# Cosine attention and a low-rank mixer: batch 1 in key tiles of 128, batch 2's quarter slots together, other planned distances, a narrower last piece

## The chip, the cores and the metric

The kernel runs on one core of a Trainium2 chip. The metric is the device time of one execution in microseconds. Before the change it is 580.38 us, the median of six runs that lie between 580.11 and 580.61. The engines are named as in the profile: PE is the tensor engine, PEld its weight loads, DVE the vector engine, ACT the scalar engine, POOL and SP the engines that here mostly issue DMAs.

## What is computed

```python
# q, k, v: (8 batches, 12 heads, 448 rows, 64), float32; tau = 0.1
q_n = q / (norm(q) + 1e-6);  k_n = k / (norm(k) + 1e-6)
attn = softmax(q_n @ k_n.T / tau)
x = attn @ v                       # heads side by side: (8, 448, 768)
# U: (448, 32), V: (32, 448), w_ch1: (768, 3072), w_ch2: (3072, 768)
h = x.T @ U @ V                    # mixes the 448 rows through rank 32
u = x + h.T
out = u + relu(u @ w_ch1) @ w_ch2
```

The kernel works in bfloat16 with float32 sums. Since the rows of q and k have length one, the kernel takes exp of the scores without their maximum.

## The kernel before

**A planner writes the order.** The program first collects operations (`Op`), each with an engine, an assumed duration, the operations that it depends on, and the buffers (`Slot` of a `Ring`) that it takes and gives back. `Plan.run` then runs a list scheduling over the five engines and emits the instructions in the order of planned starts. On the chip each engine keeps that order; if an operand comes later than planned, the engine stands still and all that is behind it waits. PE has several streams in a fixed priority: transposes, score bursts, value products, low-rank sums, and last the MLP (`pe_mlp`), which fills what the others leave. DVE, ACT and SP take the ready operation of lowest `prio`. POOL has one stream, `pool_q`, in the order of the program text.

**Planned distances.** `ready_at` lets a PE operation start no earlier than the end of an operand from another engine plus 0.1 plus `op.safe`, and the same for a buffer that comes free. `plan.safe` is set before operations are added: 0.1 for the start, 0.8 while batch 1's loads and norms are added, then (lines 1140 to 1147) 0.6 for batch 1's attention, 0.8 for that of later batches and 0.25 for all MLPs. `LATE`, 8.0, is the planned time from the end of a load's transfer to its landing for q and k of batches from 1 on and for their v (batch 0 has 2.5 and `VLATE`). The transfers themselves are planned in one queue, 1.24 us for a load of q or k.

**Attention.** Heads go in six pairs. Three loads of q and three of k bring four heads each per batch (`load_qk`). `stats` squares, sums and scales them (ACT or DVE; DVE alone for batch 1), with priority 4 from batch 1 on, and batch 1's squares come after the last product of batch 0. `norm` writes normalized q and k; they are transposed on PE for batches 0 and 1 (L477) and by DMA for the rest (L636). A **slot** is one tile of keys of one head pair: two matmuls of 64 rows by 448 columns (L682), one for each head, and one exp over both (L700). Keys are cut in one of two ways:

- For batches below `WIDE` (2) in four tiles of 112 keys: 24 slots a batch.
- From `WIDE` on in three tiles of 128, and a last one of 64 keys, which two pairs share. This **quarter slot** has four matmuls of 64 by 64 tiles (`parts`), and its other half of v is set to zero. That makes 18 full and 3 quarter slots. v then comes in ten loads instead of four (`load_v`), and its tile gets ones and zeros once by `set_v_tiles` (five memsets) instead of `set_v` (one).

Slots are issued in **bursts** (`BURST`: 1, 2, then 3 for each batch), and `groups_of` puts them in order. For batches from `TB` (3) on the three quarter slots come first, as a burst of their own, and their exps go into a ring of their own (`r_tail`); below `TB` the quarter slot stands behind the full ones of its two pairs. From batch 2 on, a burst waits in the plan for a certain MLP product of the batch before. Scores take double PSUM banks from `r_sc`: (0, 1), (2, 3), (4, 5). `values` multiplies exps by v (L727, 16 matmuls of 65 columns for each head, the last column being the sum), taking a bank from `r_av`, `r_av2` or `r_av3`, and DVE divides (L756, L758).

**Low-rank sums and MLP.** `stage0` computes A = x.T U (L811) and adds A V to x: for batch 1 in three column parts with one matmul (L861) and one DVE addition (L875, L870) per tile, each a PE operation waiting for DVE, and then transposes u on PE. Batches 0 and 1, 2 and 3 and so on share 7 row tiles of 128: the even one has three, the odd one four. `mlp` runs 24 x 6 products with the first weight (L938, 384 or 512 columns), relu (L961 on ACT, L963 on DVE), then for each row tile and each half of the 768 columns 24 products with the second weight (L974), a DVE addition (L985) and stores (L999). The last of the 14 x 4 half tiles is cut in two pieces of 192 columns; stores of pieces narrower than 384 columns and of fewer than 112 rows go to ACT's queue, all others to SP's.

**Order around the start.** POOL's stream is: q and k of batch 0, v of batch 0, half of the first weight, q and k of batch 1 with the rest of the first weight between, v of batch 1, the last q and k of batch 1, eight slices of the second weight, then q, k and v of batch 2.

Of the kernel before, what the change touches and what calls it, by code (L numbers as in the profile page):

```python
# [269 lines left out]
def kernel(  # L270
# [18 lines left out]
    NPAIR = H // 2  # L289
    CC = C // 128  # L290
    NC = F // 128
    CH = C // 2
    SC = 4
    SCH = S // SC
# [1 line left out]
    root_tau = float(tau) ** 0.5  # L296
    EPS = 1e-6
    PE_BATCHES = 2
    LATE, VLATE = 8.0, 2.8
    BURST = [1] + [2] + [3] * 6  # L300
    SPOTS = {8: [(6,)] * 7 + [()], 6: [(5, 17), (10,), (6,), (6,), (6,), (6,)]}
    WIDE = 2
    TB = 3
    RAW_KEYS = {(0, 0), (0, 1)}
    FILL = 0.7

# [78 lines left out]
    r_av3 = bank_ring([(5,), (4,), (3,), (2,), (1,), (0,)], 2, (4, D + 8))  # L385
    r_av2 = bank_ring([(5,), (4,), (3,), (2,), (1,), (0,), (6,)], 2, (4, D + 8))
    r_up = bank_ring([(7,), (6,), (5,), (4,), (3,), (2,), (1,), (0,)], 4)
    r_out = bank_ring([(7,), (6,), (5,), (4,)], 4)
    r_warm = bank_ring([(4,)], 1)
    r_sc1 = bank_ring([(0,), (2,), (1,), (3,)], 4)  # L390
# [21 lines left out]
    plan = Plan()  # L412
# [166 lines left out]

    def stats(b, h0, h1, ld, ops, lo, hold=(), then=()):  # L580

        pr = 0.3 + 0.03 * h0 if b == 0 else 4
        inv = Slot(r_inv, sum(1 + 2 * SC if (b, p) in RAW_KEYS else 2 for p in range(h0 // 2, h1 // 2)))
        o, _, _ = scales(b, h0, h1, ld, ops, lo, (0, 1), inv, pr, "ACT/DVE" if b != 1 else "DVE", hold, then)
        for p in range(h0 // 2, h1 // 2):
            o_ = norm(b, p, ld, lo + 2 * p - h0, inv, 2 * p - h0, {0: o, 1: o}, pr, {1: [ops[1]]})
        return o_
# [76 lines left out]
    def scores(b, slots, then=()):  # L664

        off = PAD * (b % 2)
        scs = [Slot(r_sc, 2 if (b, p) in RAW_KEYS else 1) for p, _ in slots]
        sets = {p: got[b, p, "qkT"] for p in members(b, slots)}
        ready = []
        for x in sets.values():  # L670
            ready += x[1]
        ready += then
        into = []
        for p, c in slots:
            of, r, n = (tails, r_tail, 4) if b >= TB and c == SC - 1 else (attns, r_attn, 2 if b < WIDE or p % 2 or b >= TB else 4)
            into.append(of.setdefault((b, p), (Slot(r, n), [])))

        def score():
            for (p, c), sc in zip(slots, scs):
                for hh, q_, n0, w, out in parts(b, p, c, sc):  # L680
                    qkT, r = sets[q_][0], slice(D * hh, D * hh + D)
                    nc.tensor.matmul(out=out, lhsT=qkT.tile.rearrange("p b s -> p (b s)")[r, n0:n0 + w],  # L682
                                     rhs=qkT.tile[r, SC:2 * SC, :].rearrange("p c s -> p (c s)"),
                                     start=True, stop=True)
        kinds = [b >= WIDE and c == SC - 1 for _, c in slots]
        o = plan.add(Op("PE", 0.2 + pe_t(S) * len(slots) + 0.12 * sum(x != y for x, y in zip(kinds, kinds[1:])), score, deps=ready, acq=scs + [x[0] for n, x in enumerate(into) if x not in into[:n]],
                        rel=[x[0] for x in sets.values()]), pe_first if b == 0 else pe_sc)
        o.big = len(slots) > 2
        if o.big:
            bursts.setdefault(b, []).append(o)  # L690
        for (p, c), sc, (attn, exps) in zip(slots, scs, into):
            _, _, (inv, a, scaled) = sets[p]
            if (b, p) in RAW_KEYS:
                for hh in range(2):
                    exps.append(plan.add(Op("ACT", act_t(S, 0.143), lambda sc=sc, c=c, hh=hh, attn=attn, inv=inv, a=a: nc.scalar.activation(  # L695
                        out=attn.tile[0:SCH, c, hh, off:off + S], in_=sc.tile[0:SCH, hh, 0:S], func=AF.Exp,
                        scale=inv.tile[:, 1, a + hh, c:c + 1]), deps=[o, scaled], acq=[attn],
                        rel=[sc, inv], prio=0.1)))
                continue
            exps.append(plan.add(Op("ACT", act_t(2 * S, 0.08), lambda sc=sc, c=c, attn=attn: nc.scalar.activation(  # L700
                out=attn.tile[:, :, off:off + S] if b >= TB and c == SC - 1 else
                attn.tile[0:SCH if b < WIDE else 128, c, :, off:off + S],
                in_=sc.tile[0:SCH if b < WIDE else 128, :, 0:S], func=AF.Exp),
                deps=[o], acq=[attn], rel=[sc], prio=0.1 if b == 0 else 1)))

    def values(b, p, X):
        off = PAD * (b % 2)
        attn, exps = attns[b, p]
        even, kp, tail = attn, SCH, None
        if b >= WIDE:  # L710
            kp = 128
            if b >= TB:
                tail, more = tails[b, p - p % 2]
                exps = exps + more
            elif p % 2:
                even = attns[b, p - 1][0]
                exps = exps + attns[b, p - 1][1]
        last_exp[b] = exps[-1]
        if b == 0 and p == 0:
            last_exp["first"] = [exps[0]]  # L720
        muls = []
        heads = []
        for hh in range(2):
            heads.append((Slot(r_av3 if b >= 3 else r_av2 if BURST[b] > 2 else r_av if b else r_av5 if p == NPAIR - 1 else r_av0, 1), Slot(r_rd, 1)))

        def product(h, hh, t, j, av, start):
            nc.tensor.matmul(out=av.tile[:, t, 0:D + 1],  # L727
                             lhsT=tail.tile[:, hh, 128 * t:128 * (t + 1)] if tail and j == SC - 1 else
                             (attn if j < SC - 1 else even).tile[0:kp, j, hh, 128 * t:128 * (t + 1)],
                             rhs=v_t[b % 2][0:kp, h, j, 0:D + 1], start=start, stop=(j == SC - 1),  # L730
                             skip_group_check=ends)
        ends = b == 0 and p == NPAIR - 1
        ready = attn_set + v_set[b]
        if ends:
            for j in range(SC):
                for hh, (av, rd) in enumerate(list(heads)):
                    h = 2 * p + hh

                    def fn(h=h, hh=hh, j=j, av=av):
                        for t in range(4):  # L740
                            product(h, hh, t, j, av, j == 0 and t == 0)
                    o = plan.add(Op("PE", 4 * 0.033, fn, deps=[exps[j]] + got[b, h, "v"] + ready,
                                    acq=[av] if j == 0 else [], rel=[attn] if j == SC - 1 else []), pe_av)
                    if j == SC - 1:
                        heads[hh] += (o,)
        for hh in range(2):
            h = 2 * p + hh
            av, rd = heads[hh][:2]
            o = heads[hh][-1]
            for t in () if ends else range(4):  # L750
                for j in range(SC):
                    first, last = t == 0 and j == 0, t == 3 and j == SC - 1
                    o = plan.add(Op("PE", 0.033 if b < 2 else 0.0305, lambda t=t, j=j, h=h, hh=hh, av=av: product(h, hh, t, j, av, j == 0),
                        deps=exps + got[b, h, "v"] + ready if first else (), acq=[av] if first else [],
                        rel=([attn, tail] if tail else [attn] if even is attn else [attn, even]) if last else []), pe_av)
            r = plan.add(Op("DVE", 0.20, lambda av=av, rd=rd: nc.vector.reciprocal(  # L756
                out=rd.tile, in_=av.tile[:, :, D:D + 1]), deps=[o], acq=[rd], prio=1))
            muls.append(plan.add(Op("DVE", dve_t(256), lambda av=av, rd=rd, h=h: nc.vector.tensor_mul(  # L758
                X.tile[:, :, h * D:(h + 1) * D], av.tile[:, :, 0:D],
                rd.tile.to_broadcast([128, 4, D])), deps=[r],  # L760
                acq=[X], rel=[av, rd], prio=1)))
        last_av[b, p] = o
        return muls
# [153 lines left out]
    def mlp(b, us, uT, ut):  # L917
# [4 lines left out]
        work = [(i, t, c0, c0 + CH) for i, t in enumerate(tiles) for c0 in (0, CH)]  # L922
        if b == B - 1:
            i, t, c0, c1 = work.pop()
            mid = (c0 + c1) // 2
            work += [(i, t, c0, mid), (i, t, mid, c1)]
            us[i].uses += 1
            us[i].left += 1
# [39 lines left out]
        for group in groups:  # L968
# [12 lines left out]
            for (i, t, c0, c1), mm in zip(group, mms):  # L981
# [6 lines left out]
                for bb in (b - par, b - par + 1):  # L988
# [3 lines left out]
                        continue  # L992
                    for nn, j, p0, p1 in segments(lo - o0, hi - o0):
                        r0 = nn + o0 - 128 * t
                        by = "ACT" if w < CH and p1 - p0 < SCH else "SP"
                        O.uses += 1
                        O.left += 1
                        plan.add(Op(by, 0.1, lambda bb=bb, j=j, p0=p0, p1=p1, r0=r0, O=O, c0=c0, c1=c1, by=by:
# [139 lines left out]
    w2_ops.append(load_w2(len(w2_ops), 2 * NW))  # L1138
    w2_ops.append(load_w2(len(w2_ops), 2 * NW))
    for b in range(1, B):  # L1140
        plan.safe = 0.6 if b == 1 else 0.8
        state[b] = att(b)
        if b + 1 < B:
            for h0, h1 in THIRDS:
                go(b + 1, h0, h1)
            load_v(b + 1)
    plan.safe = 0.25
    for b in range(B):
        mlp(b, *state[b])

# [45 lines left out]
```

## Time and profile before

| Quantity | Value |
|---|---|
| Median of six runs | 580.38 us (580.11 to 580.61) |
| The profiled execution's own time | 579.87 us |
| Its span, first to last instruction | 578.1 us, 11714 instructions |
| L938, 1152 products with the first weight | 232.3 us busy |
| L974, 1368 products with the second weight | 232.0 us busy |
| L727, 1536 value products | 58.2 us busy |
| L682, 384 score matmuls | 47.7 us busy |
| L700, 166 exps on ACT | 141.6 us busy, 917 ns each |
| q and k loads, 224 KB | 5.5 and 6.0 us from issue to landing (median) |
| v loads of 168 KB | 9.9 us (median) |
| Stores of 168 KB | 2.2 us (median) |

The page divides the span in 40 slices of 14.5 us; a 9 in an engine's row means 90% or more busy. In a list of groups, "x1152 | 232.3, 353" is the count, the busy time in us, and the mean ns of one. Matmuls are pipelined, so the recorded length of one is longer than the distance to the next start. In a timeline a row is a start, a length in us, the engine, the line, and out<-in with its shape; the brackets at its end hold idle time and what ended it. "64*128" ahead of a shape is the part of the PE array that the matmul uses.

### The profile page before, as it was taken

The page shows a single profiled execution, that of the slowest core. Times are in us where ns is not written, and L with a number is a line of the kernel's source. Part 1 is how long each engine was busy: PE and PEld are TensorE (multiplying, and loading weights), DVE is VectorE, ACT ScalarE, POOL GpSimd, SP SyncE. Part 2 cuts the span into 40 slices and gives each one's busy share as a digit, 9 for nine tenths or more (in the row PEclk, how much of TensorE's full clock was granted, in tenths as well). Part 3 has the DMA queues.
Part 4 walks back from the last instruction along what each step waited for, and adds up shares of the span by engine and source line. Part 5 has one row for each costly group of instructions (what it writes and reads, how often), then busy time and mean ns, then how long its engine had stood idle before and what let it go on. Part 6 is the DMA issues. An engine that isn't in the chain of part 4 may idle for free.

```text
span 578.1 us, 11714 instructions
## 1 busy us (share of the span) xinstructions
PE 569.9 (99%) x4871; PEld 326.7 (57%) x4871; DVE 287.6 (50%) x683; ACT 288.9 (50%) x478; POOL 92.8 (16%) x134
## 2 busy tenths in 40 slices
PE   8899999999999999999999999999999999999997
PEld 6565556445555665555455655555455656654565
DVE  8989829999665775468256740344012340100011
ACT  7967754668517651656546445443445344024200
POOL 8234240160050104011401030000000000000000
PEclk9999999999999999999999999999999999999999
DMA  9999992997595719572947373440041100310011
GB/s 157 200 207 191 210 167 65 147 134 106 92 114 127 99 26 142 110 94 35 97 97 121 76 49 66 93 77 1 0 69 33 38 14 15 83 40 1 4 51 57
DMA packets 133430, 50.70 MB, mean 88 GB/s; under 512 B 98304, under 2 KB 133376, under 8 KB 133376
## 3 DMA queue, kind: packets, MB, share of 16 engines
q0 software_dynamic: 72256, 25.73, 39.2%
q1 hardware_dynamic: 61056, 24.19, 20.4%
q8 instruction: 38, 0.62, 0.5%
q14 instruction: 16, 0.13, 0.1%
q10 hardware_dynamic: 64, 0.02, 0.0%
HBM read 52.25 MB, written 11.01 MB: 109 GB/s over the span
## 4 chain that ended last, share of the span: by engine, by line
PE 94%; DVE 3%; ACT 1%; DMA 0%; issue 0%; DVEq 0%
PE bank L974 38%; PE bank L938 38%; PE bank L727 8%; PE bank L682 6%; PE bank L861 2%; DVE xn L621 1%; PE bank L477 1%; DVE ss L553 1%; PE bank L811 1%; ACT attn L695 1%; DMA raw_uv<-in_q_dram 0%; DVE qkT L1015 0%; ACT sq L547 0%; PE bank L782 0%; DVE X_sb L758 0%
## 5 line engine op out<-in xcount | busy, mean ns | idle before, releaser
L938 PE MATMUL bank<-uT,w_sb 128*128 128x512 bf16 (+1 forms) x1152 | 232.3, 353 | 0.0
L974 PE MATMUL bank<-w_sb,relu 128*128 128x384 bf16 (+1 forms) x1368 | 232.0, 324 | 0.3 <-DVE X_sb L758 0.2
L700 ACT ACTIVATE attn<-bank 128x896 bf16<-128x896 f32 (+1 forms) x166 | 141.6, 917 | 85.7 <-PE bank L682 85.5
L974 PEld LDWEIGHTS <-relu 128*128 128x128 bf16 x1368 | 128.4, 98 | 91.9 <-issue 14.2
L938 PEld LDWEIGHTS <-w_sb 128*128 128x128 bf16 x1152 | 108.7, 98 | 101.0 <-issue 7.2
L961 ACT ACTIVATE relu<-bank 128x384 bf16<-128x384 f32 (+1 forms) x161 | 87.6, 545 | 133.5 <-PE bank L938 133.0
L985 DVE TENSOR_TENSOR O_sb<-bank,u_nat 128x384 f32<-128x384 f32 (+1 forms) x57 | 31.2, 549 | 189.7 <-PE bank L974 165.8
L553 DVE TENSOR_REDUCE ss<-sq 112x8 f32<-112x512 bf16 x96 | 62.7, 673 | 1.8 <-ACT sq L547 1.1
L727 PEld LDWEIGHTS <-attn 128*128 128x128 bf16 (+1 forms) x1536 | 55.0, 97 | 11.6 <-issue 3.2
L621 DVE TENSOR_TENSOR xn<-qk_nat,inv 112x512 bf16<-112x512 bf16 x93 | 60.4, 681 | 0.1
L727 PE MATMUL bank<-v_nat,attn 128*128 128x65 bf16 (+1 forms) x1536 | 58.2, 193 | 0.5 <-DMA v_nat<-in_v_dram 0.4
L682 PE MATMUL bank<-qkT 64*128 64x448 bf16 (+1 forms) x384 | 47.7, 355 | 1.3 <-ACT attn L695 0.6
L499 POOL DMA_DIRECT2D qk_nat<-in_q_dram x24 | 17.3, 723 | 152.2 <-issue 40.7
L758 DVE TENSOR_TENSOR X_sb<-bank,rd 128x256 bf16<-128x256 f32 x96 | 39.6, 417 | 1.6
L547 ACT ACTIVATE sq<-qk_nat 112x512 bf16<-112x512 bf16 x54 | 32.8, 632 | 9.7 <-DVE ss L553 9.4
L522 POOL DMA_DIRECT2D v_nat<-in_v_dram x36 | 26.5, 743 | 69.1 <-PE bank L727 64.3
L756 DVE RECIPROCAL rd<-bank 128x4 f32<-128x4 f32 x96 | 16.7, 177 | 41.6 <-PE bank L727 36.8
L875 DVE TENSOR_TENSOR u_nat<-bank,X_sb 128x384 bf16<-128x384 f32 (+2 forms) x45 | 22.0, 526 | 12.1 <-PE bank L861 11.8
L682 PEld LDWEIGHTS <-qkT 64*128 64x128 bf16 (+1 forms) x384 | 13.1, 96 | 24.7 <-issue 19.0
L963 DVE TENSOR_SCALAR relu<-bank 128x384 bf16<-128x384 f32 (+1 forms) x31 | 19.2, 618 | 14.8 <-PE bank L938 14.6
L499 POOL DMA_DIRECT2D qk_nat<-in_k_dram x24 | 16.8, 702 | 4.8 <-DMA w_sb<-in_moe_w_ch_dram 3.7
L549 DVE TENSOR_TENSOR sq<-qk_nat 112x512 bf16<-112x512 bf16 x40 | 16.0, 418 | 1.3 <-DMA qk_nat<-in_q_dram 1.1
(59 smaller groups left out, 186.6 us busy)
## 6 DMA issues: line engine op xcount, KB each, us to landing
qk_nat<-in_q_dram POOLq DMA_DIRECT2D x23, 224.0 KB, 5.5
qk_nat<-in_k_dram POOLq DMA_DIRECT2D x23, 224.0 KB, 6.0
w_sb<-in_moe_w_ch_dram POOLq DMA_DIRECT2D x4, 1152.0 KB, 20.7
w_sb<-in_moe_w_ch_dram POOLq DMA_DIRECT2D x8, 576.0 KB, 16.1
out_dram<-O_sb SPq DMA_DIRECT2D x15, 168.0 KB, 2.2
v_nat<-in_v_dram POOLq DMA_DIRECT2D x14, 168.0 KB, 9.9
out_dram<-O_sb SPq DMA_DIRECT2D x16, 144.0 KB, 2.1
out_dram<-O_sb SPq DMA_DIRECT2D x16, 120.0 KB, 1.9
```

What stands on the lines that cost most here:

```text
L499: ops = [load(lambda i=i, src=src: nc.gpsimd.dma_start(out=ld.tile[:, i, lo:lo + h1 - h0, :], in_=src[b, h0:h1].rearrange("h (s c) d -> s ...
L547: nc.scalar.activation(out=y, in_=x, func=AF.Square)
L553: lambda i=i, a0=a0, a1=a1, sq=sq: nc.vector.reduce_sum(ss.tile[:, i, a0:a1, :].rearrange("p h c -> p (h c)"), sq.tile[:, 0:a1 - a0, :].re ...
L621: nc.vector.tensor_mul(dst, src, sc)
L682: nc.tensor.matmul(out=out, lhsT=qkT.tile.rearrange("p b s -> p (b s)")[r, n0:n0 + w], rhs=qkT.tile[r, SC:2 * SC, :].rearrange("p c s -> p ...
L700: exps.append(plan.add(Op("ACT", act_t(2 * S, 0.08), lambda sc=sc, c=c, attn=attn: nc.scalar.activation(out=attn.tile[:, :, off:off + S] i ...
L727: nc.tensor.matmul(out=av.tile[:, t, 0:D + 1], lhsT=tail.tile[:, hh, 128 * t:128 * (t + 1)] if tail and j == SC - 1 else (attn if j < SC - ...
L758: muls.append(plan.add(Op("DVE", dve_t(256), lambda av=av, rd=rd, h=h: nc.vector.tensor_mul(X.tile[:, :, h * D:(h + 1) * D], av.tile[:, :, ...
L938: o = plan.add(Op("PE", pe_t(n), lambda cc=cc: nc.tensor.matmul(out=mm.tile[:, 0:n], lhsT=w1_sb[:, cc, f * 128:(f + 1) * 128], rhs=uT.tile ...
L961: nc.scalar.activation(out=relu.tile[:, f, 0:n], in_=mm.tile[:, 0:n], func=AF.Relu)
L974: nc.tensor.matmul(out=mm.tile[:, 0:c1 - c0], lhsT=relu.tile[:, f, i * 128:(i + 1) * 128], rhs=w2_t[:, f, c0:c1], start=(f == 0), stop=(f ...
L985: nc.vector.tensor_add(out=O.tile[:, 0:w], in0=mm.tile[:, 0:w], in1=us[i].tile[:, c0:c1]),
```

## The change

Batch 1 takes the 128-key tiles (`WIDE` 1), with score banks from a ring of two double banks, (0, 1) and (2, 3), and value banks from `r_av3`; batch 2 issues its three quarter slots first in one burst (`TB` 2). `LATE` is 4.0. The priority of batch 1's squares and norms is 2 instead of 4. `plan.safe` is 0.05 for batch 1's attention, 0.5 for later ones and 0.1 for the MLPs. The last half tile is cut into pieces of 288 and 96 columns, and both stores of the 96-column piece go to SP's queue.

```diff
-    LATE, VLATE = 8.0, 2.8
+    LATE, VLATE = 4.0, 2.8
...
-    WIDE = 2
-    TB = 3
+    WIDE = 1
+    TB = 2
...
+    r_scb = bank_ring([(0, 1), (2, 3)], 2)
...
-        pr = 0.3 + 0.03 * h0 if b == 0 else 4
+        pr = 0.3 + 0.03 * h0 if b == 0 else 2 if b == 1 else 4
...
-        scs = [Slot(r_sc, 2 if (b, p) in RAW_KEYS else 1) for p, _ in slots]
+        scs = [Slot(r_scb if b == 1 else r_sc, 2 if (b, p) in RAW_KEYS else 1) for p, _ in slots]
...
-            heads.append((Slot(r_av3 if b >= 3 else r_av2 if BURST[b] > 2 else r_av if b else r_av5 if p == NPAIR - 1 else r_av0, 1), Slot(r_rd, 1)))
+            heads.append((Slot(r_av3 if b >= 1 else r_av2 if BURST[b] > 2 else r_av if b else r_av5 if p == NPAIR - 1 else r_av0, 1), Slot(r_rd, 1)))
...
-            mid = (c0 + c1) // 2
+            mid = c1 - 96
...
-                        by = "ACT" if w < CH and p1 - p0 < SCH else "SP"
+                        by = "ACT" if 96 < w < CH and p1 - p0 < SCH else "SP"
...
-        plan.safe = 0.6 if b == 1 else 0.8
+        plan.safe = .05 if b == 1 else .5
...
-    plan.safe = 0.25
+    plan.safe = .1
```

By `load_v` and the lines around 1120, `WIDE` 1 also makes batch 1's v ten loads, its set-up `set_v_tiles`, and takes away the second set-up of that tile after batch 1's value products; the tile of batches 0 and 2 is still set anew after batch 0.

## The prediction

> **What bounds the kernel now.** I read the page's first two parts, then the busy time by stretches, then the tensor engine's timeline at single places.
>
> ```profile
> PE 569.9 (99%) x4871; PEld 326.7 (57%) x4871; DVE 287.6 (50%) x683; ACT 288.9 (50%) x478; POOL 92.8 (16%) x134
> PE   8899999999999999999999999999999999999997
> PEclk9999999999999999999999999999999999999999
> ```
>
> PE is busy for 99% of the span at the full granted clock; its only unfilled slices are the first two and the last. A busy time may hide gaps, because a 384-column matmul is recorded for about 0.33 us while the next starts 0.163 us later. So I also measured from start to start. From 38.41 us, where the chain of waits becomes an unbroken row of L938 and L974, to the last matmul, 384 columns take 163 ns (160 at 2.4 columns per ns, plus 3) and 512 columns 216 ns. What is left above that is of two kinds: the price of entering and leaving a score burst, and a few waits. Everything else (attention, norms, loads, stores) is laid beside these matmuls. Hence only four things can move the end: the tensor engine's own work, its waits, the start up to 38 us, and what follows the last matmul.
>
> ```profile
> 113.02 0.74 PE L682 MATMUL bank<-qkT 64*128 64x448 bf16 x6
> 113.69 0.82 PE L938 MATMUL bank<-uT,w_sb 128*128 128x512 bf16 x3
> ...
> 117.69 0.86 PE L682 MATMUL bank<-qkT 64*128 64x448 bf16 x8
> 118.48 1.04 PE L938 MATMUL bank<-uT,w_sb 128*128 128x512 bf16 x4
> ...
> 171.75 0.76 PE L682 MATMUL bank<-qkT 64*64 64x448 bf16 x12
> 172.45 0.99 PE L974 MATMUL bank<-w_sb,relu 128*128 128x384 bf16 x5
> ```
>
> All three are bursts of three slots. The first has three full slots (64*128 tiles) and holds the engine from 113.02 to 113.69, the second two full slots and a quarter slot (64*64), from 117.69 to 118.48, the third, of batch 3, three quarter slots, from 171.75 to 172.45. A slot streams 448 columns, 448/2.4 = 0.187 us, for its two or four matmuls run beside each other. Three make 0.56; the rest of 0.67 is leaving the 64-row tiling (0.09), and the gap before the burst shows 0.095 more for entering it. Going from full to quarter slots inside a burst costs 0.09 again; leaving from 64*64 costs 0.116 rather than 0.092.
>
> ```profile
> 60.00:75.00 15.00, 14.61 (x157) 8.64 (x155) 10.69 (x28) 11.35 (x18) 3.74 (x5) 1.00 1.18 208
> 75.00:90.00 15.00, 15.00 (x149) 8.40 (x148) 7.33 (x19) 9.76 (x16) 6.00 (x9) 1.00 1.32 128
> 90.00:105.00 15.00, 14.99 (x144) 9.57 (x142) 14.67 (x41) 4.45 (x8) 1.44 (x2) 1.00 0.33 80
> 105.00:120.00 15.00, 15.00 (x80) 6.12 (x79) 14.18 (x29) 12.30 (x21) 3.65 (x5) 1.00 0.99 150
> ```
>
> The columns are the stretch, its length, then busy us of PE, PEld, DVE, ACT and POOL. DVE is half idle from 75 to 90 us and full from 90 to 120. The waits of PE after the start lie here:
>
> ```profile
> 71.26 0.33 PE L974 MATMUL bank<-w_sb,relu 128*128 128x384 bf16 x1
> 71.74 0.95 PE L974 MATMUL bank<-w_sb,relu 128*128 128x384 bf16 x3 [0.15 <-DVE X_sb L758]
> ```
>
> From 71.26 the next should start at 71.42; it starts at 71.74, 0.32 late, and inside the x3 there is another gap of 0.30. With 0.15 before L727 at 62.30 and 0.165 and 0.17 before L861 at 94.61 and 96.03 (both behind DVE's u_nat) the waits come to 1.1 us. After 97 us I find none.
>
> **Part by part.** *Key tiles of 128 in batch 1 (WIDE 1).* Its 24 slots become 18 full and 3 quarter slots: 3 x 0.187 = 0.56 off. Bursts of two go from 12 to 11: one entry and exit less, 0.187 off. Two of the bursts now mix full and quarter (0.09 each on) and three leave from 64*64 (0.024 each on). Sum: -0.56 - 0.19 + 0.18 + 0.07 = **-0.50**. ACT loses three exps of 0.92 (L700), DVE nothing on that account; both are off the path here. The value products stay 192, of 128 rows instead of 112: 32 of L727 take 0.97 us from 122.97 with 128 rows, 30 ns each, and with 112 rows their spacing is the same 29 ns.
>
> *Batch 2's quarter slots in one burst (TB 2).* Still seven bursts, but no mixed ones: 3 x 0.09 off, and two exits from 64*64 less (0.05): **-0.32**. The new first burst needs the transposed keys of all six pairs. In the trace the last one is issued at 117.33 and lands at 122.2, while the first burst ran at 108.14. If nothing moves, bursts start 14 us later. What covers it: the trace leaves holes in this row (117.69 to 129.17, 134.05 to 146.46); from 122.5 on, seven bursts at the 4.6 us of neighbours end at 150, against a last burst at 150.97 now. Batch 2's upward products start only at 183.28. Cost nothing; without that cover, a late batch stops PE one for one.
>
> *Loads.* V of batch 1 goes from 4 loads of 0.94 us on POOL to 10 of about 0.73: 3.5 us more of POOL, in a stretch (24.67 to 40.5) where POOL stands idle for some 12 us behind the queue; the second weight's eight slices and batch 2's q and k are behind it in the stream. Ten pieces for batch 2 took 5.25 us from the landing before them (82.19) to their own last (87.44), four for batch 1 took 4.44 (45.86 to 50.30), so what follows lands up to 0.8 us later. The last slice of the second weight landed at 75.18 and is first used about 10 us after L974 begins at 71.3. Hidden. SP's stream has no new step there.
>
> *Ones and zeros of v.* The set-up of batch 1's tile grows from one memset (0.10 at 28.34) to five (0.09, two of 0.06, two of 0.24), +0.6 us on DVE, and the same five at 97.70, in the full stretch, vanish. At 28.3 DVE has gaps of 0.21, 0.24 and 0.29 ahead of the next three reciprocals; behind the memset wait L756 and L758, which free the bank for the next value product. That product is late by up to 0.4 once, but ACT's eight exps in a row (27.71 to 34.35) set that stretch. Taken as 0, at most +0.4.
>
> *Planned distances.* LATE 4 instead of 8 and batch 1's priority 2 put no work on any engine; they order it. q and k land 3.6 to 6.8 us after issue in the later batches, about what 0.71 of issue, 1.24 of transfer and 4 give; at worst DVE stands for under 1 us, with relus done 1.26 us or more ahead of the third product after them. For batch 2 it lets squares move from the full stretch into 75 to 90 us. The spare time behind operands falls from 0.6 to 0.05 in batch 1, 0.8 to 0.5 later, 0.25 to 0.1 in the MLP. Today a value product starts at least 1.09 us after the last exp that it needs in batch 1, 1.13 in batch 2; less 0.55 and 0.3 that leaves 0.54 and 0.83, so waits behind ACT are not to be expected. Behind DVE there were waits in spite of 0.6. The bounds: all 1.1 us goes (DVE's load is spread, batch 1 finishes earlier, its sums leave the full stretch), or each handover is late by what the margin hid. I take half gone, **-0.55**, nearer to the first, since DVE has 7.7 us free just ahead of the full stretch.
>
> *Last piece.* 24 x 384 columns stay, cut 288+96 instead of 192+192. Here a rule speaks against the change. The row first: L727 streams only 65 columns behind a 128-column weight load recorded at 97 ns, and starts every 30 ns. The Trainium skill, "TensorE: Matmul & The Clock Gate", section "Back-to-back issue gap", gives a sustained 81 ns per matmul at 128 columns where each has its own weight load. By it 96 columns take some 81 ns, 24 x 39 = 0.9 us lost; by the row 96/2.4 + 2.5 = 42.5, nothing lost. I take the row. After the last matmul:
>
> ```profile
> 574.55 0.36 DVE L985 TENSOR_TENSOR O_sb<-bank,u_nat 128x192 f32<-128x192 f32 x1 [1.62 <-PE bank L974]
> ```
>
> At 384 columns it takes 0.558, so 96 take 0.26: -0.10. Then SP issued the 112-row store at 574.94 (landed 577.04, 2.10) and ACT the 16-row one (1.76). Now SP issues both, short one first; two issues follow each other by 0.366: +0.37. Half the bytes land after 1.76 to 2.10; I take 1.9: -0.2. Sum **+0.06**, between -0.07 and +0.27. The skill's "DMA: Bandwidth & Descriptors" ("Specifications") puts pieces under 512 B, as these 384 B rows are, below line rate; no row here shows such a store, and it argues for the upper end.
>
> **Sum.** -0.50 - 0.32 - 0.55 + 0.06 = -1.3 us. The profiled execution took 579.87, its span 578.1, and the median of the runs is 580.38; the difference carries over: **579.1**, own range 578.2 to 579.2.
>
> **Rivals.** *(1) The waits stay as they are.* DVE is as full as before at batch 1's sums, thinner margins eat what smoothing gives: -0.82 + 0.06 = 579.6 (579.2 to 581.5). For it: margins shrink everywhere. Against: the free DVE time.
> *(2) Slower: batch 1's handovers from DVE to PE wait.* The place is its low-rank sums (L811, L861) and the transposes behind them, some 15 steps of PE behind DVE. At 0.6 of margin they were 0.17 late, so DVE was 0.77 behind; at 0.05 such a step stops PE for 0.72, and with it every MLP matmul behind it. Three such stops cancel the gain of 1.3 and add 0.9; five make it 582.4. From the fourth on it decides; I price it at 582. Against: lateness does not start anew after each stop, so one stop may be all.
> *(3) It does not do what it says:* the planner builds the order anew from these numbers, and the batch-2 burst could be pushed late enough to hold the MLP. It would need over 20 us of the slack above; folded into (2).
>
> **Chances.** Forecast 0.48, rival 1 0.32, rival 2 with 3 0.20. A measurement of this kernel tells 0.2% (1.16 us) from no change, so the forecast lies just on the faster side: faster 0.48, same 0.32, slower 0.20. The range, 578.1 to 581.7, goes from nearly all waits gone to the first stops of rival 2.
>
> **What would show it.** 21 slots in 11 bursts for batch 1; in batch 2 one x12 burst of 64*64 and six of x6; gaps of PE from 38 to 100 us under 0.6 us in all; DVE above 7.3 us in the stretch before batch 1's sums and below 14.7 in theirs; 24 matmuls of 96 columns in about 1.0 us; two SP issues 0.37 apart at the end. It is wrong if L861 or L477 show starts late by over 0.3 us several times, if the matmuls of 96 columns come 80 ns apart, or if L938 of batch 2 waits for uT.

## The result and the profile after

The changed kernel takes 578.96 us (median of 17 runs, 578.62 to 579.88), the kernel before, run beside it, 580.31 us. The ratio is 0.9977, with a 95% interval of 0.997 to 0.9983: 1.3 us faster. 579.1 was forecast. The sum was right; two of its terms were wrong by about 0.3 and 0.4 us and cancelled each other.

A time here is longer than the span of its execution: by 1.79 us (median) in the kernel before, by 2.13 in the changed one. So some 0.3 us of what the spans gained does not show in the times. Kernels below that differ from the changed one only in planned distances, or in the queue of one store, have from 1.77 to 2.10. What makes this difference is not known; where two times lie close to each other, median spans are given too (576.8 us for the changed kernel).

The page of the changed kernel, first and second part:

```profile
span 576.6 us, 11735 instructions
PE 568.7 (99%) x4871; PEld 326.4 (57%) x4871; DVE 290.1 (50%) x694; ACT 280.6 (49%) x463; POOL 96.2 (17%) x140
PE   8899999999999999999999999999999999999997
PEclk9999999999999999999999999999999999999999
```

PE still fills the span at the full clock, so the same four places are asked again. From the ring that the change adds on, line numbers are one higher than before: L938 is now L939, and so on. The timeline of PE in the changed kernel, at three bursts:

```profile
60.36 0.68 PE L683 MATMUL bank<-qkT 64*128 64x448 bf16 x6
...
122.60 0.76 PE L683 MATMUL bank<-qkT 64*64 64x448 bf16 x12
123.30 1.04 PE L939 MATMUL bank<-uT,w_sb 128*128 128x512 bf16 x4
...
127.50 0.74 PE L683 MATMUL bank<-qkT 64*128 64x448 bf16 x6
```

The first is a burst of batch 1 that holds a full and a quarter slot (two matmuls and four), the second batch 2's three quarter slots in one burst, the third a later burst of batch 2, of three full slots. The busy time by stretches of the changed kernel (PE, PEld, DVE, ACT, POOL):

```profile
60.00:75.00 15.00, 15.00 (x187) 9.38 (x186) 10.42 (x30) 9.55 (x15) 3.74 (x6) 1.00 1.16 209
75.00:90.00 15.00, 15.00 (x150) 8.35 (x148) 10.80 (x26) 8.06 (x12) 6.94 (x10) 1.00 1.62 192
90.00:105.00 15.00, 14.83 (x143) 9.68 (x141) 14.64 (x38) 5.00 (x9) 2.16 (x4) 1.00 0.94 119
105.00:120.00 15.00, 15.00 (x71) 6.84 (x70) 14.29 (x29) 11.40 (x25) 6.53 (x10) 1.00 0.94 130
```

DVE has indeed moved work into 75 to 90 us (10.80 for 7.33), but it is as full afterwards as it was.

Measured from start to start over all of PE's matmuls, from the first product with the first weight on, the two profiled executions compare like this (a tiling switch is an entry into a burst, an exit, or a change inside it):

| Term, us | before | after | difference | forecast |
|---|---|---|---|---|
| First product with the first weight starts | 36.67 | 37.12 | +0.46 | 0 |
| Columns of score slots | 28.00 | 27.44 | -0.56 | -0.56 |
| Tiling switches | 12.62 (131) | 12.35 (128) | -0.27 | -0.26 |
| Waits over 0.03 us | 1.09 | 0.38 | -0.70 | -0.55 |
| From the last DVE addition's start to the end | 3.54 | 3.21 | -0.34 | +0.06 |

The rest of the 1.48 us by which the spans of these two executions differ is below 0.1. Their times differ by 1.14.

**The start.** Of the 0.46, 0.14 is there at the first norm already (4.75 us before, 4.89 after), before anything that the change touches. The other 0.32 comes in at one place. In the kernel before, the reciprocal stands behind one memset and the six value products run through:

```profile
28.34 0.10 DVE L1021 MEMSET v_nat<- 112x48 uint32 x1
28.65 0.18 DVE L756 RECIPROCAL rd<-bank 128x4 f32<-128x4 f32 x1 [0.21 <-PE bank L727]
29.17 0.36 PE L727 MATMUL bank<-v_nat,attn 112*128 112x65 bf16 x6
```

In the changed kernel, first DVE, then PE:

```profile
28.46 0.09 DVE L1026 MEMSET v_nat<- 128x36 uint32 x1
28.49 0.06 DVE L1028 MEMSET v_nat<- 64x6 uint32 x1
28.52 0.24 DVE L1029 MEMSET v_nat<- 64x216 uint32 x1
...
28.88 0.24 DVE L1029 MEMSET v_nat<- 64x216 uint32 x1
29.15 0.18 DVE L757 RECIPROCAL rd<-bank 128x4 f32<-128x4 f32 x1
29.36 0.42 DVE L759 TENSOR_TENSOR X_sb<-bank,rd 128x256 bf16<-128x256 f32 x1
```

```profile
29.31 0.33 PE L728 MATMUL bank<-v_nat,attn 112*128 112x65 bf16 x5
29.84 0.19 PE L728 MATMUL bank<-v_nat,attn 112*128 112x65 bf16 x1 [0.21 <-DVE X_sb L759]
```

The reciprocal stands behind five memsets, so the division ends at 29.79, the value bank comes free, and only then does the sixth value product start: at 29.84, where 29.48 was due (29.34 in the kernel before, plus the 0.14). From the first of these six products to the first L939 it is 7.49 us before and 7.82 after.

**The waits.** After 38 us one of 0.33 is left before 300 us, before L862 of batch 1. The second of the two L975 starts at 96.63, so L862 was due at 96.79 and came at 97.12:

```profile
96.47 0.49 PE L975 MATMUL bank<-w_sb,relu 128*128 128x384 bf16 x2
96.78 0.29 DVE L876 TENSOR_TENSOR u_nat<-bank,X_sb 128x128 bf16<-128x128 f32 x1
...
97.12 0.22 PE L862 MATMUL bank<-A_sb,V_sb 128*128 128x128 bf16 x1 [0.17 <-DVE u_nat L876]
```

**The end.** The last two additions on DVE:

```profile
572.38 0.46 DVE L986 TENSOR_TENSOR O_sb<-bank,u_nat 128x288 f32<-128x288 f32 x1 [2.38 <-PE bank L975]
573.40 0.26 DVE L986 TENSOR_TENSOR O_sb<-bank,u_nat 128x96 f32<-128x96 f32 x1 [0.56 <-PE bank L975]
```

The 24 matmuls of 96 columns start 42.5 ns apart. SP issues the two stores, the 16-row one first, at 573.69 and 574.06, 0.366 apart; they land after 1.47 and 1.57 us.

### The profile page after: what moved, and what is told of

Read it like the earlier page. It is cut to its first block, busy times and chain, and to the rows that moved or that the text cites. A ratio compares the mean times of both kernels' runs of the same rounds, so it can differ in the third digit from the quotient of the medians.

```text
span 576.6 us, 11735 instructions
## 1 busy us (share of the span) xinstructions
PE 568.7 (99%) x4871; PEld 326.4 (57%) x4871; DVE 290.1 (50%) x694; ACT 280.6 (49%) x463; POOL 96.2 (17%) x140
## 4 chain that ended last, share of the span: by engine, by line
PE 93%; DVE 4%; ACT 1%; DMA 0%; issue 0%; DVEq 0%
PE bank L939 38%; PE bank L975 38%; PE bank L728 8%; PE bank L683 6%; PE bank L862 1%; DVE xn L622 1%; DVE ss L554 1%; PE bank L478 1%; ACT attn L696 1%; PE bank L812 1%; DMA raw_uv<-in_q_dram 0%; DVE X_sb L759 0%; DVE u_nat L876 0%; ACT sq L548 0%; DVE qkT L1016 0%
## 5 line engine op out<-in xcount | busy, mean ns | idle before, releaser
L975 PE MATMUL bank<-w_sb,relu 128*128 128x384 bf16 (+2 forms) x1368 | 233.4, 324 | 0.0
L939 PE MATMUL bank<-uT,w_sb 128*128 128x512 bf16 (+1 forms) x1152 | 229.7, 353 | 0.0
L975 PEld LDWEIGHTS <-relu 128*128 128x128 bf16 x1368 | 127.3, 98 | 90.9 <-issue 13.4
L701 ACT ACTIVATE attn<-bank 128x896 bf16<-128x896 f32 (+1 forms) x163 | 138.9, 917 | 73.1 <-PE bank L683 72.9
L939 PEld LDWEIGHTS <-w_sb 128*128 128x128 bf16 x1152 | 109.8, 98 | 103.8 <-issue 7.1
L962 ACT ACTIVATE relu<-bank 128x384 bf16<-128x384 f32 (+1 forms) x164 | 89.2, 544 | 127.3 <-PE bank L939 126.6
L986 DVE TENSOR_TENSOR O_sb<-bank,u_nat 128x384 f32<-128x384 f32 (+2 forms) x57 | 31.0, 547 | 196.7 <-PE bank L975 171.5
L728 PE MATMUL bank<-v_nat,attn 128*128 128x65 bf16 (+1 forms) x1536 | 56.9, 193 | 0.2 <-DVE X_sb L759 0.2
L523 POOL DMA_DIRECT2D v_nat<-in_v_dram x42 | 31.0, 745 | 73.8 <-PE bank L728 40.7
L548 ACT ACTIVATE sq<-qk_nat 112x512 bf16<-112x512 bf16 x42 | 25.6, 631 | 23.4 <-DMA qk_nat<-in_q_dram 12.0
L550 DVE TENSOR_TENSOR sq<-qk_nat 112x512 bf16<-112x512 bf16 x52 | 20.4, 419 | 11.1 <-DMA qk_nat<-in_q_dram 10.8
L964 DVE TENSOR_SCALAR relu<-bank 128x384 bf16<-128x384 f32 (+1 forms) x28 | 17.3, 619 | 11.7 <-PE bank L939 11.4
L528 POOL DMA_DIRECT2D v_nat<-in_v_dram x28 | 17.4, 628 | 8.8 <-DMA w_sb<-in_moe_w_ch_dram 4.8
```

What stands on the lines that cost most here:

```text
L523: ops = [load(lambda j=j, r0=r0, c=c, s0=s0, s1=s1: nc.gpsimd.dma_start(out=v_t[b % 2][r0:r0 + s1 - s0, :, j, 0:D], in_=src[c, s0:s1]), (s ...
L548: nc.scalar.activation(out=y, in_=x, func=AF.Square)
L728: nc.tensor.matmul(out=av.tile[:, t, 0:D + 1], lhsT=tail.tile[:, hh, 128 * t:128 * (t + 1)] if tail and j == SC - 1 else (attn if j < SC - ...
L939: o = plan.add(Op("PE", pe_t(n), lambda cc=cc: nc.tensor.matmul(out=mm.tile[:, 0:n], lhsT=w1_sb[:, cc, f * 128:(f + 1) * 128], rhs=uT.tile ...
L962: nc.scalar.activation(out=relu.tile[:, f, 0:n], in_=mm.tile[:, 0:n], func=AF.Relu)
L975: nc.tensor.matmul(out=mm.tile[:, 0:c1 - c0], lhsT=relu.tile[:, f, i * 128:(i + 1) * 128], rhs=w2_t[:, f, c0:c1], start=(f == 0), stop=(f ...
```

## The experiments

Each kernel is given as an edit of the changed kernel, or of the kernel before where that is said. "Ratio" is to the kernel before, with its 95% interval.

### The set-up of batch 1's v tile later

```diff
-        old = [last_av.get((b - 2, p)) for p in range(NPAIR)] + (v_set[b] if WIDE <= b < WIDE + 2 else [])
+        old = [last_av.get((b - 2, p)) for p in range(NPAIR)] + (v_set[b] if b == 2 else [])
...
-    v_set[1] = [fill(lambda: (set_v if WIDE > 1 else set_v_tiles)(v_t[1]), 1000, prio=3, deps=late)]
...
+    v_set[1] = [fill(lambda: set_v_tiles(v_t[1]), 1000, prio=3.9, deps=after)]
```

So batch 1's loads of v no longer wait for the memsets either.

> The changed kernel with one edit: the five set-up memsets of batch 1's v tile come after batch 0's value products instead of at 28.5 us, ahead of the reciprocal that frees a value bank. Theory: those 0.6 us of DVE stop PE by 0.32 us at the start, once, and nothing takes it up later; so the gap of 0.37 before L728 near 29.8 goes, the first L939 comes at about 36.8 instead of 37.12, and the time is 0.3 us below the changed kernel (about 578.65). Rival: the start is set by the eight exps in a row and the delay is only shifted slack, or the memsets find another place where DVE is full: first L939 may move, but the time stays within 0.1 us of the changed kernel.

579.35 us, ratio 0.9984 (0.9976 to 0.9991). The gap at 29.8 was gone: from the first of the six value products (29.43) to the first L939 (36.92) it was 7.49 us again. But the memsets then fell among the landings of the same tile, and DVE was held there:

```profile
51.25 0.24 DVE L1029 MEMSET v_nat<- 64x216 uint32 x1 [0.28 <-DMA v_nat<-in_v_dram]
...
51.61 0.24 DVE L1029 MEMSET v_nat<- 64x216 uint32 x1
51.88 0.39 DVE L1016 COPY qkT<-bank 128x448 bf16<-128x448 bf16 x1
```

The copy of keys behind them freed a bank late, and PE stood for 0.42 us at 52.33. It stood for another 0.39 at 131.6, where the changed kernel has no wait. So the theory of the 0.32 at the start held, and the rival's "another place" as well: nothing was won (median span 577.2 us).

### The last stores: width and queue

One kernel keeps the 96 columns and gives the short store back to ACT:

```diff
-                        by = "ACT" if 96 < w < CH and p1 - p0 < SCH else "SP"
+                        by = "ACT" if w < CH and p1 - p0 < SCH else "SP"
```

> The changed kernel with one edit: the short store of the last 96-column piece goes to ACT's queue again, beside SP's long one. Theory A (the queue): the two queues hold each other up; the last landing is about 2.0 us after its issue as before the change, so that from the start of the last DVE addition to the end of the span it is about 3.4 us (3.54 before, less 0.10 of addition), 0.2 longer than the 3.205 of the changed kernel. Theory B (the width): half the bytes land sooner on any queue, and both issues start together; then it is 2.85 to 2.95, 0.3 shorter than the changed kernel.

The other has 192 and 192 columns and one queue for the last piece:

```diff
-            mid = c1 - 96
+            mid = (c0 + c1) // 2
...
-                        by = "ACT" if 96 < w < CH and p1 - p0 < SCH else "SP"
+                        by = "ACT" if w < CH and c1 < C and p1 - p0 < SCH else "SP"
```

> The changed kernel with the last half tile cut in 192 and 192 columns again, but both stores of the last piece on SP's queue. Theory A (the queue): stores on one queue land 1.5 to 1.6 us after issue whatever their width; from the start of the last DVE addition to the end 3.3 us, that is the 3.205 of the changed kernel plus 0.10 for the longer addition. Theory B (the width): the 112-row store of 192 columns takes 1.8 to 2.1 us after an issue that is 0.37 late; 3.6 to 3.9 us, above the 3.54 of the kernel before.

| Last piece | Long store lands after | Short store lands after | From the addition's start to the end |
|---|---|---|---|
| 192 columns, SP and ACT (before) | 1.77 | 2.10 (ACT) | 3.54 |
| The same, in the two kernels of "Each half alone" | 1.77 | 1.94 (ACT) | 3.37 |
| 192 columns, SP alone | 1.81 | 1.36 | 3.55 |
| 96 columns, SP alone (changed) | 1.57 | 1.47 | 3.21 |
| 96 columns, SP and ACT | 1.53 | 1.69 (ACT) | 3.03 |

The last two rows as the profile gives them, the changed kernel first (KB, us to landing):

```profile
out_dram<-O_sb SPq DMA_DIRECT2D x1, 42.0 KB, 1.6
out_dram<-O_sb SPq DMA_DIRECT2D x1, 6.0 KB, 1.5
...
out_dram<-O_sb SPq DMA_DIRECT2D x1, 42.0 KB, 1.5
out_dram<-O_sb ACTq DMA_DIRECT2D x1, 6.0 KB, 1.7
```

Times are 578.44 us (ratio 0.9965, 0.9951 to 0.9978) for the narrow piece on two queues and 579.37 (0.9981, 0.9974 to 0.9987) for the wide one on one; their intervals overlap with the changed kernel's (median spans 576.6 and 577.3), so the verdict rests on the table. The width does it: 0.34 less on one queue, and on two 0.34 less than in two of the three traces, 0.51 less than in the third, that of the kernel before. That is nearer to theory B than to A both times, though a little outside B's figures (3.03 for 2.85 to 2.95, 3.55 for 3.6 to 3.9). One queue costs 0.17 for the narrow piece, and 0.17 for the wide one by the same two traces. So of the 0.34 by which the end became shorter, half may be that the one trace of the kernel before had a late landing (2.10 for 1.94).

### The old distances with the new tiles

```diff
-    LATE, VLATE = 4.0, 2.8
+    LATE, VLATE = 8.0, 2.8
...
-        pr = 0.3 + 0.03 * h0 if b == 0 else 2 if b == 1 else 4
+        pr = 0.3 + 0.03 * h0 if b == 0 else 4
...
-        plan.safe = .05 if b == 1 else .5
+        plan.safe = 0.6 if b == 1 else 0.8
...
-    plan.safe = .1
+    plan.safe = 0.25
```

> The changed kernel with the planned distances and the priority of before (LATE 8, priority 4, spare times 0.6, 0.8 and 0.25); tiles, rings and last piece as changed. Theory: the distances took 0.7 us of PE's waits away by letting DVE do batch 2's squares from 75 to 90 us; so PE's waits between 38 and 100 us are 0.9 to 1.2 us instead of 0.4, DVE is busy for 7 to 8 us from 75 to 90, and the time is 579.6 to 579.8. Rival 1: the tiles removed the waits (batch 1 has fewer slots and ends earlier): waits stay at about 0.4 and the time at 579.0. Rival 2: with the quarter slots of batch 2 first and loads planned late, batch 2 comes too late and PE stands: time above 581.

586.81 us, ratio 1.0116 (1.0097 to 1.0134). None of the three had expected this place: not batch 2 but batch 1 came too late. The value products of its last head pair, called the last value product from here on, started at 98.8 us (91.0 in the changed kernel), its low-rank sums behind that, and the MLP of batch 0 was finished before batch 1's u was ready. In this trace the granted clock was also 0.50 from 19 to 26 us, as in the trace of the narrow piece on two queues, whose edit touches only stores; its first L939 came at 38.91 us, so some 1.8 of the 7.8 us stand there already, and its time, 589.31, lies above the median. By stretches (PE first, then PEld, DVE, ACT, POOL, and the granted clock behind POOL):

```profile
105.00:112.50 7.50, 2.92 (x35) 1.99 (x35) 7.38 (x22) 4.13 (x8) 1.39 (x2) 0.92 0.55 90
112.50:118.00 5.50, 5.28 (x13) 1.93 (x14) 4.47 (x8) 1.89 (x4) 1.66 (x3) 0.50 0.64 105
```

PE is busy for 2.92 of 7.5 us, and then the clock is 0.50 for 5.5 us: thirteen matmuls in a stretch that takes twenty-five at 216 ns. The stop is paid twice: 4.6 us of standing, then some 2.7 of slow work.

### Which distance it is

First the spare times alone taken back:

```diff
-        plan.safe = .05 if b == 1 else .5
+        plan.safe = 0.6 if b == 1 else 0.8
...
-    plan.safe = .1
+    plan.safe = 0.25
```

> The changed kernel with the spare times of before (0.6, 0.8, 0.25), but LATE 4 and priority 2 as changed. Taking all distances back gave 586.8 us, because batch 1's low-rank sums came after the MLP of batch 0 had run out. Theory M (margins): batch 1's attention is a chain of short handovers between PE and ACT through two double banks, so 0.55 us more at each of about 11 bursts puts it some 6 us later; the stop near 100 to 112 us comes back by more than half, time 583 to 587. Theory L (loads): the planned landing of batch 1's last q and k and of batch 2 set the lateness; then this kernel stays within 1 us of the changed one, below 580.

589.27 us, ratio 1.0158 (1.0144 to 1.0172): theory M. The last value product of batch 1 started at 99.9 us, 8.9 later, and L939 of batch 1 at 113.32; there the clock at the start was full. Then LATE alone:

```diff
-    LATE, VLATE = 4.0, 2.8
+    LATE, VLATE = 8.0, 2.8
```

> The changed kernel with LATE 8 alone taken back. Theory M (margins): the last value product of batch 1 comes less than 2 us later than the 91 us of the changed kernel and no long stop of PE follows; time within 1 us of it, below 580; DVE is less busy from 75 to 90 us and PE's waits at batch 1's sums are about 0.5 us longer. Theory L (loads): batch 1's last three pairs come about 4 us later, the sums fall behind the end of batch 0's MLP, and PE stands for several us as when all distances were old; time 583 to 587.

582.19 us, ratio 1.0032 (1.0024 to 1.004). Batch 1 was as early as in the changed kernel (90.6 us), so theory L is out for it. But the time is not theory M's either: PE stood in another place. Its timeline:

```profile
180.36 0.80 PE L683 MATMUL bank<-qkT 64*128 64x448 bf16 x6
183.44 0.65 PE L939 MATMUL bank<-uT,w_sb 128*128 128x384 bf16 x3 [2.28 <-DMA uT<-u_nat]
```

Here the MLP of batch 1 has ended and batch 2's transposed u has not landed. The first burst of batch 2 needs all keys; with loads planned late it came at 126.45 us instead of 122.60, and the last u landed at 183.30 instead of 178.07. The trace is of an execution of 580.79 us, the shortest of fifteen; its stop is 2.36 us from start to start, and what adds the other 1.4 us to the median is not shown. The clock stayed at 1.00 behind this stop. To test the part of the burst, the quarter slots went back behind their pairs, with LATE 8 kept:

```diff
-    TB = 2
+    TB = 3
```

> The changed kernel with LATE 8 and with batch 2's quarter slots behind their pairs again (TB 3). LATE 8 alone made batch 2's transposed u land at 183.3 us, and L939 of batch 2 stood 2.33 us. Theory Q: the first burst of quarter slots needs all six pairs' keys, and that made batch 2 late; without it its bursts begin near 108 us as in the kernel before, its u lands before 178 us, no stop is left there, and the time is 579.0 to 579.6 (0.3 of tiling switches above the changed kernel). Rival: late loads alone make batch 2 late; the stop of 1.5 us or more near 183 us stays and the time is above 581.

578.81 us, ratio 0.9971 (0.9961 to 0.9982), median span 577.0: theory Q. The first burst came at 107.42, u landed at 172.87, no stop was left. This run also says something about the waits:

```profile
75.00:90.00 15.00, 15.00 (x148) 8.30 (x144) 6.99 (x19) 8.35 (x13) 6.96 (x10) 1.00 1.67 189
90.00:105.00 15.00, 15.00 (x145) 9.84 (x143) 14.68 (x37) 5.65 (x11) 1.45 (x2) 1.00 0.48 93
```

DVE has 6.99 us in the stretch before batch 1's sums and is full in theirs, as before the change, and PE has no wait at all there. The priority taken back to 4 did not matter either:

```diff
-        pr = 0.3 + 0.03 * h0 if b == 0 else 2 if b == 1 else 4
+        pr = 0.3 + 0.03 * h0 if b == 0 else 4
```

> The changed kernel with batch 1's squares and norms at priority 4 again. Theory: the priority only orders DVE in 37 to 68 us; batch 1's last keys come up to 1 us later, its last value product stays before 93 us, and the time is within 0.5 us of the changed kernel. Rival: the wait of 0.3 to 0.5 us at the first products with the second weight near 72 us, which was there before the change and with all old distances and not with priority 2, comes back, and batch 1's last value product falls 3 us or more later with a stop near 105 us: time over 581.

578.58 us, ratio 0.9967 (0.9954 to 0.998), with a median span of 576.8, that of the changed kernel. Batch 1's last value product started at 92.6, and the waits were 0.44 us in all, 0.19 of them near 70 us.

Last, the small spare time for batch 1's attention only:

```diff
-        plan.safe = .05 if b == 1 else .5
+        plan.safe = .05 if b == 1 else 0.8
...
-    plan.safe = .1
+    plan.safe = 0.25
```

> The changed kernel with spare time 0.05 for batch 1's attention only; 0.8 for later batches and 0.25 for the MLP as before the change. Theory: what keeps the tiles' batch 1 in time is its own margin; its last value product then comes near 91 us, there is no stop of over 1 us near 105 us, and the time is within 0.5 us of the changed kernel (578.5 to 579.5). Rival: the MLP's or the later batches' margins share in it; then the last value product comes after 94 us and PE stops again for several us (time over 582).

580.88 us, ratio 1.0005 (0.9997 to 1.0013), so neither. The last value product started at 85.9, before the 91.0 of the changed kernel, and no long stop came near 105. But the waits were 2.6 us, the longest of them where a value product was put ahead of an exp that it needed:

```profile
82.66 0.26 PE L728 MATMUL bank<-v_nat,attn 128*128 128x65 bf16 x3
82.87 0.90 ACT L701 ACTIVATE attn<-bank 128x896 bf16<-128x896 f32 x1
...
83.82 0.54 PE L728 MATMUL bank<-v_nat,attn 128*128 128x65 bf16 x12 [0.90 <-ACT attn L701]
```

ACT was late behind a square that waited for DVE. That is what a spare time of 0.05 risks, in an order where an engine happens to be late.

### Each half alone, on the kernel before

The distances and the priority without the tiles (the lines of the old distances above, taken the other way):

> The kernel before with the new distances and priority alone (LATE 4, priority 2, spare times 0.05, 0.5, 0.1); tiles and last piece as before. If the distances take away waits by themselves, PE's waits after 38 us fall from 1.1 to about 0.4 us and the time to 579.6 (0.7 below). If they are good only for keeping the tiles' batch 1 in time, waits stay at 1 us or grow where the margin hid DVE's lateness (0.5 or more at L861), and the time is 580.3 to 581.5.

581.69 us, ratio 1.0024 (1.0016 to 1.0033): worse by 1.4. The trace is of the longest of its twenty executions, 583.78 us, so its waits are more than the median has: 4.1 us instead of 1.1, among them 1.06 before the projection of batch 1 at 93.8 (behind five memsets and a division on DVE), 0.62 and 0.80 before L938 at 133.8 and 204.1 (relus late behind ACT and DVE that waited for a load of q or k), and 0.61 inside a score burst at 179.2. And the tiles without the rest:

```diff
-    WIDE = 2
-    TB = 3
+    WIDE = 1
+    TB = 2
```

> The kernel before with WIDE 1 and TB 2 alone: no ring of two double banks, no other value banks, distances and last piece as before. PE's own work falls by 0.83 us (three slots and three tiling switches less). If batch 1's lateness comes from tiles with old distances whatever the banks, PE stands several us at batch 1's sums near 105 us, at half the clock for a while after, and the time is 584 to 588. If the ring of two double banks is what slows batch 1 (a burst must wait for both exps of the one before), there is no long stop here, and the time is 579.5 to 580.3.

583.47 us, ratio 1.0054 (1.004 to 1.0068), between the two expectations: PE's work fell as expected (27.44 us of slot columns, 128 switches), but the last value product of batch 1 came at 96.1 us and L938 of batch 1 at 108.2 instead of 105.5, with the clock at 0.50 for 3.4 us behind it. So the tiles make batch 1 late with the old banks too; through which of their steps is not shown.

### Both small losses taken away

The five memsets go to POOL, which stands idle there, and the short store goes to ACT's queue:

```diff
-    v_set[1] = [fill(lambda: (set_v if WIDE > 1 else set_v_tiles)(v_t[1]), 1000, prio=3, deps=late)]
...
+    v_set[1] = [plan.add(Op("POOL", 2.0, lambda: set_v_pool(v_t[1])), pool_q)]
...
-                        by = "ACT" if 96 < w < CH and p1 - p0 < SCH else "SP"
+                        by = "ACT" if w < CH and p1 - p0 < SCH else "SP"
```

`set_v_pool` is `set_v_tiles` with `nc.gpsimd.memset`; it stands behind the third load of the first weight.

> The changed kernel with two edits: the set-up memsets of batch 1's v tile go to POOL, near 15 us where it stands idle, and the short store of the last piece goes to ACT's queue. PE's order is that of the changed kernel. Theory: 0.32 us less at the start (first L939 at 36.8 or less, no wait of L728 near 29.8) and 0.17 less after the last addition (3.03 instead of 3.205), so 0.5 us below the changed kernel: 578.4 to 578.6. Rival: memsets on POOL hold up q and k loads of batch 1 behind them or slow DVE at 15 us, and the start gains nothing: 578.7 to 579.

578.46 us, ratio 0.9964 (0.9951 to 0.9976). On POOL the memsets ran from 16.12 to 17.26, inside a pause of the stream. The value products behind 29.3 us came 0.32 earlier than in the changed kernel, the first L939 at 36.80, and the end after the last addition took 2.99 us. A wait of 0.25 at 130.7 was new, though PE's order is the same. Start, end and this wait make 0.3 us, and so do the two traced spans (576.31 and 576.61). By the median times it is 0.5 us below the changed kernel, but by the median spans 0.1 (576.7), and the two intervals overlap: that step is shown by the trace, not by the times.

## Why the prediction was right, point by point

**The sum** came within 0.15 us of the measured time, in part by luck. The traces have 0.46 more at the start, 0.40 less at the end and 0.15 less in the waits than was forecast, which with the small rest makes -1.48 us in the span for the -1.31 forecast; and then 0.3 us of it did not reach the time.

**What bounds the kernel** held: every gain and loss that was traced lies in PE's own work, its waits, the start or the end.

**The tiles' and the burst's own work** (-0.50 and -0.32) came out as summed: -0.56 of columns, -0.27 of switches.

**Batch 2 later at no cost** held in the changed kernel: the first burst ran at 122.60, the last at 154.13 (150 was expected), u landed at 178.07, and L939 of batch 2 began at 181.31. The slack was 3 us, and LATE 8 used it up. The prediction (rival 3) had spoken of over 20 us; with bursts only 3.9 us later than in the changed kernel PE already stood for 2.36.

**Batch 1 later** was not in the prediction. It priced the tiles by what they add and remove; an earlier end of batch 1 stood there only as one bound of the waits, a later one not at all. That was the most expensive question of this change: with the tiles alone the last value product came 4 us later and the kernel lost 3 us. The planned distances, taken there as a matter of up to 1.1 us of waits, were what keeps the tiles in time: taking them back cost 7.9 us, the spare times alone 10.3.

**The waits, half gone** (-0.55): the size was right (-0.70), the reason fell. DVE's work moved as forecast, but without that move (LATE 8, TB 3) the waits were gone too. What removes them is not settled: LATE, the priority and TB are each excluded, since one of them or two together were taken back and 0.3 to 0.45 us of waits stayed; with old spare times there were 0.3 to 0.5 near 59 or 72 us, and with the new ones on the old tiles 4.1 in the one trace. I take it as a property of the whole order that the planner finds.

**The memsets, 0**: wrong, they cost 0.32, near the upper end of 0.4. The step that failed is the cover: eight exps in a row do not hide a delay of the value products, because the chain from division to bank to product to the next division has no slack of its own there.

**The last piece, +0.06**: it brought -0.34, outside its bounds (-0.07 to +0.27). The mis-sized term is the landing: 1.9 us were taken for the long store and it needed 1.57. The addition (-0.10) and the second issue (+0.37) came as summed. A misreading stands behind it. The prediction gave the landing at 577.04 to SP's long store; it was ACT's short one, issued beside it. SP's had landed at 576.70, 1.77 after its issue. So the long store, which the prediction let land after 2.10 us and with half the bytes after 1.9, had needed 1.77 from the start. The 96-column matmuls went by the row (42.5 ns) and not by the 81 ns that the Trainium skill ("TensorE: Matmul & The Clock Gate", "Back-to-back issue gap") gives for 128 columns. What the skill says of pieces below 512 B ("DMA: Bandwidth & Descriptors", "Specifications") is about rate, and did not decide here: on one queue the store of 112 rows of 384 B landed after 1.57 us, that of 768 B after 1.81. Whether the smaller one ran below line rate no run shows.

**Loads under 1 us late for DVE**: 1.26 at 128.4 in the changed kernel. It cost PE nothing there, and 0.10 to 0.39 at the same place in four kernels whose last piece or memsets alone differ.

**Rival 2** named a mechanism that exists, at the old tiles (4.1 us of waits in the longest execution) and with the small spare time for batch 1 alone (2.6); in the changed kernel its one late step is the 0.33 before L862. By the prediction's own steps five stops make 582.7, not 582.4 (579.1 and five times 0.72).

## What to carry to other kernels

Where one engine is full and everything else is laid beside it, price a change to a stage also by when that stage ends, against the moment at which the full engine runs out of other work; a stop there is paid twice if the clock falls. Retuned constants belong to the order they were tuned with: each half of this change alone made the kernel slower. And before a small operation is called hidden, follow the very next instructions on its engine to the buffer that they free.

## What the runs showed of the hardware

After PE had been busy for 2.92 us of 7.5, its granted clock was 0.50 for the next 5.5 us (old distances); behind a single stop of 2.36 us (LATE 8) it stayed at 1.00. The 16-row store landed later from ACT's queue than from SP's (1.94 to 2.10 against 1.36 us at 192 columns, 1.63 to 1.69 against 1.47 at 96); but on SP's queue it went out 0.37 us ahead of the long store and on ACT's beside it, so queue and company are not told apart. Five memsets that DVE did in 0.65 us as uint32 took POOL 1.14 us, the same bytes as bf16.
